# Inverse power-of-two factors for queries and keys in an attention and expert kernel

## The chip, the cores and the metric

The kernel runs on one core of a Trainium2 chip. Its engines are TensorE (PE in the profile; PEld is its loading of weights), VectorE (DVE), ScalarE (ACT), GpSimd (POOL) and SyncE (SP), which issues most of the DMAs. The metric is the device time of one execution in microseconds.

## The reference

The input x (2048 rows of 512) is normalised by rows to xn, and two branches read xn. The result is `x + A(xn) + B(xn)`.

```python
def _A_ref(x, wq, wk, wv, wo):          # H = 32 heads, Dh = 16, one key and value head
    q = (x @ wq).reshape(B, S, H, Dh).transpose(0, 2, 1, 3)
    k = x @ wk
    v = x @ wv
    scores = jnp.einsum("bhqd,bkd->bhqk", q, k) * (Dh ** -0.5)
    p = softmax(scores, axis=-1)
    o = jnp.einsum("bhqk,bkd->bhqd", p, v)
    return o.transpose(0, 2, 1, 3).reshape(B, S, H * Dh) @ wo
```

Branch B projects xn for 32 expert heads, scores each half of a projection against 64 sub-keys, takes the best two of each half, forms the best two of 4096 experts, and adds up `softmax(score) * gelu(xn . u[e]) * v[e]` over heads and chosen experts.

## The kernel before

**Start.** The normalised rows are transposed in four groups of 512 rows. `transpose_group` (L182) transposes four 128x128 blocks on TensorE into one PSUM buffer, copies them on ScalarE to a rounded high part (L193), and VectorE subtracts to get the low part (L194). `key_products` (L208) multiplies a group with the key and value weights, twelve matmuls; ScalarE copies the product (L217), squares the keys (L219) and makes a scaled copy of them in fp16 (L221). `key_rows` (L224) subtracts for the low part of the keys (L226) and puts six DMAs in line that copy them into `kaug`. For each of four blocks of query columns, `queries` (L1360) runs `query_products` (L251, twelve matmuls), `query_sq` (L260, a square on ScalarE), whatever functions are passed as `between`, `query_high` (L265, the scaled fp16 copy on ScalarE) and `query_low` (L274, the low part on VectorE, with two stores). `query_products` alternates between two PSUM buffers, so a block waits until the block two before it has gone through `query_low`.

**The factors.** Queries and keys are stored in fp16, scaled by powers of two. `weight_squares` (L289) has ScalarE square the query and key weights with a sum along each row; `scale_factors` (L297) sums over partitions with one matmul (L301), takes the root on ScalarE, and gets `sqk` (one factor for queries, one for keys) and `soft`, which takes both factors back out and holds the 1/4 of the reference. The squares stand ahead of the first `transpose_group`, and `scale_factors` ahead of the first `key_products`.

**Attention.** There are 32 units (four blocks of 512 queries, eight groups of four heads). For each unit and each of 16 blocks of 128 keys, `scores` (L406) runs two matmuls twice into a PSUM buffer of 128x1024 (two of these exist), and ScalarE takes the exponential of each (L417) with `soft`, a tile of one value per partition, as its scale. `pv` (L419) multiplies the exponentials with the values. One step of `att_steps` (L1250) holds two key blocks, thus four exponentials.

**Experts, interleaved.** Between the scores of a step the program's order lays pieces of branch B: sub-key scores (L629) with the best values (L642, L644); gathers of expert rows by POOL (L1089), dot products (L1101) and sums (L1136) on VectorE for the first half of the rows; and for the second half a dense form. That one builds a matrix of gates from one-hot rows on VectorE (L890 to L893), with small matmuls (L923) and a copy on ScalarE (L928), and then multiplies all experts (L831, L969). The dense form runs twice, once for each of the last two groups of rows. The order of instructions on every engine is written out by the program; `spent` and the costs that `yield` returns set it, and no run changes it.

Of the kernel before, what the change touches and what calls it, by code (L numbers as in the profile page):

```python
# [11 lines left out]
F32 = mybir.dt.float32  # L12
F16 = mybir.dt.float16
F32R = mybir.dt.float32r
BF16 = mybir.dt.bfloat16
I32 = mybir.dt.int32
U32 = mybir.dt.uint32
AF = mybir.ActivationFunctionType
OP = mybir.AluOpType
AX = mybir.AxisListType  # L20
# [3 lines left out]
P = 128  # L24
# [3 lines left out]
DH = 16  # L28
# [4 lines left out]
KC = D // P  # L33
# [12 lines left out]
SCALE = DH ** -0.5  # L46
LIMIT2 = 25000.0
C_IN = 0.7978845608028654
C_CUB = 0.044715 * C_IN
TOP = 1024.0  # L50
MROW = 32768.0
EXPONENT = 0x7F800000
HOLD = 44
MOST = 4.0
UNIT = 0.235
# [3 lines left out]
def tile_kernel(ctx, tc, x, wq, wkv, wo, wqT, kT, uv, ub, vb, out):  # L59
    nc = tc.nc  # L60
    pool = lambda name, **kw: ctx.enter_context(tc.tile_pool(name=name, **kw))
    dram = pool("dram", bufs=1, space=DRAM)
    const = pool("const", bufs=1)
# [4 lines left out]
    start = start_stack.enter_context(tc.tile_pool(name="start", bufs=1))  # L68
# [23 lines left out]
    wkv_f = start.tile([P, KC, 32], F32, name="wkv_f")  # L92
# [5 lines left out]
    vaug = const.tile([P, NT, 32], F32, name="vaug")  # L98
# [6 lines left out]

    mrow = start.tile([2, 512], F16, name="mrow")
    nc.gpsimd.memset(mrow, MROW)
    blk = start.tile([P, 32], BF16, name="blk")
    blk_f = start.tile([P, 32], F32, name="blk_f")
    nc.gpsimd.memset(blk_f, 1.0)  # L110
# [13 lines left out]
    xtile = lambda name: ps.tile([P, 512], F32, name=name, tag="x", bufs=3)  # L124
    stile = lambda name: ps.tile([P, 2, 512], F32, name=name, tag="s")
# [24 lines left out]
    def norm_stats(g, js):  # L150
        if g not in MV:
            MV[g] = start.tile([P, GT, 2], F32, name="mv", bufs=2)
        for j in js:
            st = start.tile([P, 6], F32, name="st", bufs=2)
            nc.vector.bn_stats(st, XS[g][j])
            nc.vector.bn_aggr(MV[g][:, j, :], st)
        if js[-1] == GT - 1:
            v = start.tile([P, GT], F32, name="ve", bufs=2)
            nc.vector.tensor_scalar(v, MV[g][:, :, 1], 1e-5, None, op0=OP.add)
            sd = start.tile([P, GT], F32, name="sd", bufs=2)  # L160
            nc.scalar.activation(sd, v, AF.Sqrt)
            RS[g] = v, sd
# [19 lines left out]
    def transpose_group(g, ks=range(KC)):  # L182
        first = g < 1
        for k in ks:
            if first:
                xt = big.tile([P, 2, 512], F32R, name="xt", bufs=4)
                XT.append(xt)
            else:
                xt = start.tile([P, 2, 512], F32R, name="xtt", tag="xtt", bufs=6)
            p = xtile("ptr")  # L190
            for j in range(GT):
                nc.tensor.transpose(p[:, j * P:(j + 1) * P], XN[g * GT + j][:, k * P:(k + 1) * P], ident)
            nc.scalar.copy(xt[:, 0, :], p)  # L193
            nc.vector.tensor_tensor(out=xt[:, 1, :], in0=p, in1=xt[:, 0, :], op=OP.subtract)  # L194
            XK.setdefault(g, []).append(xt)
            if not first:
                BULK.append(lambda k=k, xt=xt: nc.sync.dma_start(d_xt[g - 1][k], raw(xt[:])))
# [2 lines left out]

    FIRST = ((0, 0), (1, 0), (0, 1))
    sqk = const.tile([P, 2], F32, name="sqk")
    soft = const.tile([P, 1], F32, name="soft")
    qmax = const.tile([P, NGRP], F32, name="qmax")
    kmax = small.tile([32, NGRP], F32, name="kmax", bufs=1)
    KV, SQ, PQ, PK, QT = {}, {}, {}, {}, {}

    def key_products(g):  # L208
        p = stile("pkv")[:32, 0, :]
        n = 0  # L210
        for a, b in FIRST:
            for k in range(KC):
                w = (wkv_h, wkv_l)[a]
                nc.tensor.matmul(p, w[:, k, :], XK[g][k][:, b, :], start=n == 0, stop=n == 11)
                n += 1
        kv = big.tile([32, 512], F32, name="kv", tag="wk", bufs=NWK)
        nc.scalar.copy(kv, p)  # L217
        sq = start.tile([16, 512], BF16, name="ksq", tag="sq", bufs=3)
        nc.scalar.activation(sq, kv[:16, :], AF.Square)  # L219
        kh = big.tile([32, 2, 512], F16, name="kh", tag="wk", bufs=NWK)  # L220
        nc.scalar.activation(kh[:, 0, :], kv, AF.Copy, scale=sqk[:32, 1:2])  # L221
        KV[g] = kv, kh, sq

    def key_rows(g):  # L224
        kv, kh, sq = KV[g]
        nc.vector.scalar_tensor_tensor(kh[:, 1, :], kv, sqk[:32, 1:2], kh[:, 0, :], op0=OP.mult, op1=OP.subtract)  # L226
        c = slice(g * 512, (g + 1) * 512)

        def copies():
            for base in (0, 64):  # L230
                nc.sync.dma_start(kaug[base:base + 16, c], kh[:16, 0, :])
                nc.sync.dma_start(kaug[base + 16:base + 32, c], kh[:16, 1, :])
                nc.sync.dma_start(kaug[base + 32:base + 48, c], kh[:16, 0, :])

        store(copies)
# [7 lines left out]
                              pt[:, :P].rearrange("p (c n) -> p c n", n=32)[:, :, DH:])  # L243

    def key_squares(g):
        kv, kh, sq = KV.pop(g)
        p = xtile("pks")
        nc.tensor.matmul(p[:32, :], blk[:16, 0:1].to_broadcast([16, 32]), sq, start=True, stop=True)
        nc.vector.reduce_max(kmax[:, g:g + 1], p[:32, :], axis=AX.X)
# [37 lines left out]
            nc.vector.reduce_max(qmax[:, g:g + 1], PK.pop(g), axis=AX.X)  # L287

    def weight_squares():  # L289
        cols = PK["cols"] = start.tile([P, 3], F32, name="cols")  # L290
        waste = stile("pws")
        for i in range(2):
            nc.scalar.activation(waste, wraws[i], AF.Square, accum_out=cols[:, i:i + 1])
        nc.scalar.activation(waste[:, 0, :KC * DH].rearrange("p (k n) -> p k n", k=KC), wkv_f[:, :, :DH], AF.Square,
                             accum_out=cols[:, 2:3])

    def scale_factors():  # L297

        ones = vaug[:, :4, :].rearrange("p t n -> p (t n)")
        p = xtile("pws")  # L300
        nc.tensor.matmul(p[:, :3], ones, PK.pop("cols"), start=True, stop=True)  # L301
        total = start.tile([P, 2], F32, name="total")
        nc.vector.tensor_copy(total, p[:, 1:3])
        nc.vector.tensor_add(total[:, 0:1], total[:, 0:1], p[:, 0:1])
        root = start.tile([P, 2], F32, name="root")
        nc.vector.tensor_scalar(total, total, 1e-36, None, op0=OP.max)
        nc.scalar.activation(root, total, AF.Sqrt)
        nc.vector.reciprocal(root, root)
        nc.vector.tensor_single_scalar(root.bitcast(I32), root.bitcast(I32), EXPONENT, op=OP.bitwise_and)
        nc.vector.tensor_scalar(sqk, root, TOP, None, op0=OP.mult)  # L310
        back = start.tile([P, 2], F32, name="back")
        nc.vector.reciprocal(back, sqk)
        nc.vector.scalar_tensor_tensor(soft, back[:, 0:1], SCALE, back[:, 1:2], op0=OP.mult, op1=OP.mult)

    def zero_m():
        z = gtile(F16)
# [87 lines left out]
    PT, PV = {}, {}  # L404

    def scores(u, kc, i):  # L406
        p = stile("sc")
        for b in range(2):
            o = 64 * b
            nc.tensor.matmul(p[:, b, :], kaug[o:o + 64, kc * P:(kc + 1) * P], QA[u][o:o + 64, i, :],  # L410
                             start=True, stop=True)
        if (u, kc, i) not in PT:
            if late[0] is None:
                PT[u, kc, i] = gtile(F32, (P, 2, 512), "pt")
            else:
                PT[u, kc, i] = late[0].tile([P, 2, 512], F32, name="pt", tag="pt", bufs=6)
        nc.scalar.activation(PT[u, kc, i], p, AF.Exp, scale=soft)  # L417

    def pv(u, kc):  # L419
        if kc == 0:  # L420
# [114 lines left out]
    def out_ready():  # L535
        return PWO and GT * QB[PWO[0][0]] + PWO[0][1] in LIVE
# [713 lines left out]
    def att_steps(d, mid, fill):  # L1250
# [25 lines left out]
        if 0 < i < STEPS:  # L1276
            scores(u, kc + 1, 0)
            scores(u, kc + 1, 1)
        if out_ready() and (i % 128 >= HOLD and PWO[0][0] != 1 or i % 128 >= 32 and i % 4 == 0 and PWO[0][0] == 1):
            block_out()  # L1280
# [39 lines left out]
    with tc.manual_schedule(engines=ENGINES):  # L1320
        load_group(0)
        nc.sync.dma_start(wkv_f, wkv.rearrange("(k p) n -> p k n", p=P))
        wraws = []
# [19 lines left out]
                                                    in1=wqs[k][:, 0, :], op=OP.subtract)  # L1343
        for k in range(KC):
            nc.scalar.copy(wqs[k][:, 0, :], wraws[k // 2][:, k % 2, :])
        weight_squares()
        norm_apply(0)
        wq_half(0)
        wq_half(1)
        transpose_group(0)  # L1350
        wq_half(2)
        wq_half(3)
        scale_factors()

        def stores(bulk=0):
            run(STORES)
            for _ in range(min(bulk, len(BULK))):
                BULK.pop(0)()

        def queries(g, r, *between):  # L1360
            stores(2)
            query_products(g, r)
            query_sq(g, r)
            for fn in between:
                fn()
            query_high(g, r)
            query_low(g, r)

        key_products(0)
        queries(0, 0, lambda: norm_stats(1, range(2)), lambda: key_rows(0))  # L1370
        queries(0, 1, lambda: value_rows(0), lambda: query_squares(0, 0), lambda: norm_stats(1, range(2, GT)))
        queries(0, 2, lambda: key_squares(0), lambda: query_squares(0, 1), lambda: norm_apply(1))
# [190 lines left out]
```

## Time and profile before

| | us |
|---|---|
| median of 3 runs | 1848.32 |
| lowest and highest run | 1840.08, 1848.66 |
| the profiled execution | 1845.24 |
| its span | 1843.5 |
| mean granted clock of TensorE | 0.996 of full speed |

The profile is of one execution. The span runs from its first to its last instruction on the core. Rows name the line, the engine, the operation, and the tile written and read; "busy" is the time in which an engine executed. A row of waits says which engine's line stood idle and whose result ended the wait.

### The profile page before, as it was taken

To read this page: it belongs to the slowest core of one execution; us is meant where nothing else is said; L and a number is where in the kernel's file an instruction comes from. 1 tells how busy PE (TensorE), PEld (TensorE's weight loads), DVE (VectorE), ACT (ScalarE), POOL (GpSimd) and SP (SyncE) were. 2 spreads that over 40 slices of the span, in tenths; PEclk is the share of its full clock that TensorE was granted. 3 is DMA by queue.
4 is the path that set the end of the run, shared out by engine and by line. 5 is a ranking of instruction groups with operands and counts; after the bars stand their busy time and mean duration, and the time that the engine had idled before them with its cause. 6 is when DMAs were issued, how large, how long until landed. Compare 5 with 4: busy or idle time off the path is not lost.

```text
span 1843.5 us, 34938 instructions
## 1 busy us (share of the span) xinstructions
PE 1762.1 (96%) x10991; PEld 885.1 (48%) x10991; DVE 1627.5 (88%) x6386; ACT 1376.5 (75%) x1752; POOL 701.4 (38%) x921
## 2 busy tenths in 40 slices
PE   7999999999998889999999999999987899999998
PEld 4644444455554334555555544555543344555553
DVE  6749988999899967999999897899989778999994
ACT  4367766666668997888888666666689888888884
POOL 1124544435442113344344453345421124444430
PEclk9999999999999999999999999999999999999999
DMA  7489897996754767888899996877626759998882
GB/s 267 187 300 371 300 334 239 353 323 240 238 186 140 239 227 223 276 265 290 289 294 323 350 317 220 292 250 245 229 90 220 250 181 295 284 304 282 290 276 98
DMA packets 243705, 478.31 MB, mean 259 GB/s; under 512 B 93748, under 2 KB 117316, under 8 KB 243516
## 3 DMA queue, kind: packets, MB, share of 16 engines
q0 software_dynamic: 73728, 268.47, 43.2%
q1 hardware_dynamic: 169372, 206.93, 33.8%
q8 instruction: 87, 1.43, 0.3%
q14 instruction: 102, 0.84, 0.1%
q10 hardware_dynamic: 416, 0.66, 0.1%
HBM read 419.94 MB, written 51.15 MB: 256 GB/s over the span
## 4 chain that ended last, share of the span: by engine, by line
PE 67%; DVE 8%; ACT 7%; DMA 5%; issue 4%; SPq 1%; POOL 1%; another core or an unknown queue 0%; ACTq 0%; DVEq 0%; POOLq 0%
PE pv L427 19%; PE psc L629 17%; PE sc L410 12%; PE pact L831 8%; PE pout L969 7%; ACT pt L417 5%; PE pwo L525 2%; DVE xa L1136 2%; PE pw L581 1%; DVE g L1101 1%; DVE oh L890 1%; DVE i L644 1%; DMA wk<-dw 1%; DMA g<-in_uv_dram,idx 1%; ACT gst L928 1%
## 5 line engine op out<-in xcount | busy, mean ns | idle before, releaser
L417 ACT ACTIVATE pt<-sc,soft 128x1024 f32<-128x1024 f32 x1024 | 1087.9, 1123 | 336.4 <-PE sc L410 277.3
L1089 POOL DMA_INDIRECT g<-in_uv_dram,idx x512 | 563.3, 1100 | 909.5 <-DVE xa L1136 425.2
L427 PE MATMUL pv<-pt,vaug 128*32 128x512 f32 x4096 | 496.4, 602 | 0.0
L629 PE MATMUL psc<-wk,xt 128*128 128x512 f32 x1536 | 391.5, 402 | 2.7 <-DVE wk L591 1.0
L410 PE MATMUL sc<-qa,kaug 64*128 64x512 f16 x2048 | 338.6, 383 | 43.4 <-ACT pt L417 37.9
L1136 DVE SCALAR_TENSOR_TENSOR xa<-g,w,xa 128x512 f32<-128x512 f32 x512 | 374.6, 751 | 0.1
L1101 DVE CUSTOM_DVE_ANT_0 g<-g,xa 128x512 f32<-128x512 f32 x512 | 337.1, 689 | 5.6 <-DMA g<-in_uv_dram,idx 5.4
L629 PEld LDWEIGHTS psc<-wk,xt 128*128 128x128 f32 x1536 | 277.7, 188 | 96.3 <-issue 34.7
L410 PEld LDWEIGHTS <-kaug 64*128 64x128 f16 x2048 | 87.2, 94 | 403.9 <-issue 400.8
L427 PEld LDWEIGHTS pv<-pt,vaug 128*32 128x32 f32 x4096 | 107.4, 109 | 254.3 <-issue 254.3
L644 DVE FIND_INDEX8 i<-m,psc 128x8 uint32<-128x64 f32 x1024 | 207.7, 233 | 0.6 <-issue 0.6
L969 PE MATMUL pout<-wk,wd 128*128 128x512 f32 x768 | 194.9, 401 | 2.0 <-DVE gy L1012 1.1
L831 PE MATMUL pact<-xt,wk 128*128 128x512 f32 x768 | 196.5, 400 | 0.0
L969 PEld LDWEIGHTS pout<-wk,wd 128*128 128x128 f32 x768 | 140.7, 188 | 43.9 <-issue 5.6
L831 PEld LDWEIGHTS pact<-xt,wk 128*128 128x128 f32 x768 | 139.3, 188 | 42.4 <-issue 13.2
L642 DVE MAX8 m<-psc 128x8 f32<-128x64 f32 x1024 | 146.8, 221 | 14.2 <-PE psc L629 13.0
L796 DVE TENSOR_TENSOR wk<-rw,wk 128x512 fp32r<-128x512 f32 x128 | 85.9, 691 | 9.7 <-ACT wk L795 9.7
L972 DVE TENSOR_TENSOR da<-da,pout 128x512 f32<-128x512 f32 x128 | 83.0, 688 | 5.4 <-PE pout L969 5.4
L644 DVE MATCH_VALUE_LOAD i<-m,psc 128x8 f32 x1024 | 82.9, 81 | 0.0
L890 DVE TENSOR_TENSOR oh<-oh 128x2048 f16<-128x2048 f16 x64 | 78.1, 1220 | 3.4 <-ACT oh L857 1.6
L795 ACT CAST wk<-rw 128x512 fp32r<-128x512 f32 x128 | 74.3, 634 | 0.0
L1124 DVE SCALAR_TENSOR_TENSOR w<-gth,ga 128x4 f32<-128x4 f32 x128 | 20.9, 163 | 54.0 <-ACT gth L1117 48.8
(178 smaller groups left out, 1333.3 us busy)
## 6 DMA issues: line engine op xcount, KB each, us to landing
wk<-dw SPq DMA_DIRECT2D x96, 512.0 KB
wqt<-in_wqT_dram SPq DMA_DIRECT2D x32, 512.0 KB
dw<-wk SPq DMA_DIRECT2D x32, 512.0 KB
rw<-in_ub_dram SPq DMA_DIRECT2D x64, 256.0 KB
rw<-in_vb_dram SPq DMA_DIRECT2D x64, 256.0 KB
gy<-dg SPq DMA_DIRECT2D x64, 256.0 KB
dg<-gst SPq DMA_DIRECT2D x14, 928.0 KB
g<-in_uv_dram,idx POOLq DMA_INDIRECT x512
```

Source lines behind the costliest of these rows:

```text
L410: nc.tensor.matmul(p[:, b, :], kaug[o:o + 64, kc * P:(kc + 1) * P], QA[u][o:o + 64, i, :], start=True, stop=True)
L417: nc.scalar.activation(PT[u, kc, i], p, AF.Exp, scale=soft)
L427: nc.tensor.matmul(PV[u][32 * j:32 * j + 32, :], vaug[:, kc, :], pt[:, b, :], start=kc == 0, stop=kc == 15)
L629: nc.tensor.matmul(p, XT[k][:, a, j * P:(j + 1) * P], WC[n_][k][:, bb, :], start=n == 0, stop=n == 11)
L642: nc.vector.max(m8[:, jb, s, :], p[:, s * E:(s + 1) * E])
L644: nc.vector.max_index(i8[:, jb, s, :], m8[:, jb, s, :], p[:, s * E:(s + 1) * E])
L831: nc.tensor.matmul(p, us[:, a, k * P:(k + 1) * P], XT[k][:, c, :], start=n == 0, stop=n == 11)
L890: nc.vector.tensor_tensor(out=oa, in0=num(P), in1=bc(0, tb, P), op=OP.is_equal)
L969: nc.tensor.matmul(p, wd[0][:, a, j * P:(j + 1) * P], vs[:, c, :], start=n == 0, stop=n == 5)
L1089: nc.gpsimd.indirect_dma_start(out=gt, out_offset=None, in_=uv, in_offset=bass.IndirectOffsetOnAxis(ap=IDX[ph, c, ti][:, s:s + 1], axis=0))
L1101: nc.vector.tensor_tensor_reduce(u, u, XN[TPH * ph + ti], scale=1.0, scalar=0.0, op0=OP.mult, op1=OP.add, accum_out=a[:, i:i + 1])
L1136: nc.vector.scalar_tensor_tensor(acc, v, w[:, i:i + 1], acc, op0=OP.mult, op1=OP.add)
```

## The change

`weight_squares` writes the squares themselves, as bf16, without sums; it runs after the transposes of the first group. `scale_factors` runs after the first `key_products`, and sums the squares over the 512 input features with eight matmuls against a matrix of ones, so each column of the weights gets the square of its norm. It takes the largest of the query columns and of the key columns, and the fourth root of their ratio, cut to a power of two, is the queries' factor; the keys' factor is its inverse. `soft` is gone, and the exponential's scale is the number `SCALE` = 0.25. The scaled copy of the keys moves from `key_products` into `key_rows`, so in ScalarE's order it stands behind the square of the first query block.

```diff
-TOP = 1024.0
+LEAST = 1e-18
...
+    ones = start.tile([P, P], BF16, name="ones")
+    nc.gpsimd.memset(ones, 1.0)
...
-    soft = const.tile([P, 1], F32, name="soft")
...
         nc.scalar.activation(sq, kv[:16, :], AF.Square)
+        KV[g] = kv, sq
+
+    def key_rows(g):
+        kv = KV[g][0]
         kh = big.tile([32, 2, 512], F16, name="kh", tag="wk", bufs=NWK)
         nc.scalar.activation(kh[:, 0, :], kv, AF.Copy, scale=sqk[:32, 1:2])
-        KV[g] = kv, kh, sq
-
-    def key_rows(g):
-        kv, kh, sq = KV[g]
...
     def weight_squares():
-        cols = PK["cols"] = start.tile([P, 3], F32, name="cols")
-        waste = stile("pws")
+        sq = PK["wsq"] = start.tile([P, KC, 512], BF16, name="wsq")
         for i in range(2):
-            nc.scalar.activation(waste, wraws[i], AF.Square, accum_out=cols[:, i:i + 1])
-        nc.scalar.activation(waste[:, 0, :KC * DH].rearrange("p (k n) -> p k n", k=KC), wkv_f[:, :, :DH], AF.Square,
-                             accum_out=cols[:, 2:3])
+            nc.scalar.activation(sq[:, 2 * i:2 * i + 2, :], wraws[i], AF.Square)
+        sk = PK["ksq"] = start.tile([P, KC, DH], BF16, name="wksq")
+        nc.scalar.activation(sk, wkv_f[:, :, :DH], AF.Square)
 
     def scale_factors():
 
-        ones = vaug[:, :4, :].rearrange("p t n -> p (t n)")
-        p = xtile("pws")
-        nc.tensor.matmul(p[:, :3], ones, PK.pop("cols"), start=True, stop=True)
-        total = start.tile([P, 2], F32, name="total")
-        nc.vector.tensor_copy(total, p[:, 1:3])
-        nc.vector.tensor_add(total[:, 0:1], total[:, 0:1], p[:, 0:1])
-        root = start.tile([P, 2], F32, name="root")
-        nc.vector.tensor_scalar(total, total, 1e-36, None, op0=OP.max)
-        nc.scalar.activation(root, total, AF.Sqrt)
-        nc.vector.reciprocal(root, root)
-        nc.vector.tensor_single_scalar(root.bitcast(I32), root.bitcast(I32), EXPONENT, op=OP.bitwise_and)
-        nc.vector.tensor_scalar(sqk, root, TOP, None, op0=OP.mult)
-        back = start.tile([P, 2], F32, name="back")
-        nc.vector.reciprocal(back, sqk)
-        nc.vector.scalar_tensor_tensor(soft, back[:, 0:1], SCALE, back[:, 1:2], op0=OP.mult, op1=OP.mult)
+        sq, sk = PK.pop("wsq"), PK.pop("ksq")
+        p, q = xtile("pws"), xtile("pwk")
+        for k in range(KC):
+            nc.tensor.matmul(p, ones, sq[:, k, :], start=k == 0, stop=k == KC - 1)
+        for k in range(KC):
+            nc.tensor.matmul(q[:, :DH], ones, sk[:, k, :], start=k == 0, stop=k == KC - 1)
+        most = start.tile([P, 2], F32, name="most")
+        nc.vector.reduce_max(most[:, 0:1], p, axis=AX.X)
+        nc.vector.reduce_max(most[:, 1:2], q[:, :DH], axis=AX.X)
+        nc.vector.tensor_scalar(most, most, LEAST, None, op0=OP.max)
+        root = start.tile([P, 1], F32, name="root")
+        nc.vector.reciprocal(root, most[:, 0:1])
+        nc.vector.tensor_mul(root, root, most[:, 1:2])
+        nc.scalar.activation(root, root, AF.Sqrt)
+        nc.scalar.activation(root, root, AF.Sqrt)
+        nc.vector.tensor_single_scalar(sqk[:, 0:1].bitcast(I32), root.bitcast(I32), EXPONENT, op=OP.bitwise_and)
+        nc.vector.reciprocal(sqk[:, 1:2], sqk[:, 0:1])
...
-        nc.scalar.activation(PT[u, kc, i], p, AF.Exp, scale=soft)
+        nc.scalar.activation(PT[u, kc, i], p, AF.Exp, scale=SCALE)
...
-        weight_squares()
         norm_apply(0)
         wq_half(0)
         wq_half(1)
         transpose_group(0)
+        weight_squares()
         wq_half(2)
         wq_half(3)
-        scale_factors()
...
         key_products(0)
+        scale_factors()
         queries(0, 0, lambda: norm_stats(1, range(2)), lambda: key_rows(0))
```

More of the change, by code (lines that the diff above doesn't have):

```diff
@@ L245, in key_squares @@
     def key_squares(g):
-        kv, kh, sq = KV.pop(g)
+        kv, sq = KV.pop(g)
         p = xtile("pks")
```

## The prediction

> **What bounds the kernel now.** I read the page first, then the busy time by stage, then who waited for whom. Of the page, the span, PE's row and the costliest group carry the argument:
>
> ```profile
> span 1843.5 us, 34938 instructions
> PE 1762.1 (96%) x10991; PEld 885.1 (48%) x10991; DVE 1627.5 (88%) x6386; ACT 1376.5 (75%) x1752; POOL 701.4 (38%) x921
> L417 ACT ACTIVATE pt<-sc,soft 128x1024 f32<-128x1024 f32 x1024 | 1087.9, 1123 | 336.4 <-PE sc L410 277.3
> ```
>
> TensorE is busy 96% of the span and ScalarE 75%. The exponential, the line whose scale changes, is 1024 instructions and four fifths of ScalarE's work, but ScalarE sat idle 336.4 us before it, mostly waiting for TensorE. An average hides stages, so I asked for the busy time in stretches (start:end, length, then busy us and count for each engine, granted clock, DMA share):
>
> ```profile
> 900.00:1000.00 100.00, 99.18 (x583) 51.84 (x582) 98.25 (x232) 85.09 (x115) 45.51 (x39) 1.00 0.89 286
> 1100.00:1200.00 100.00, 100.00 (x568) 48.70 (x567) 85.70 (x505) 65.32 (x72) 37.01 (x56) 1.00 0.77 262
> ...
> 575.00:665.00 90.00, 72.77 (x891) 30.51 (x889) 84.30 (x165) 86.76 (x110) 16.93 (x14) 0.98 0.55 186
> 1375.00:1463.00 88.00, 71.96 (x814) 30.48 (x814) 76.13 (x152) 83.55 (x106) 16.21 (x14) 0.98 0.64 216
> ```
>
> The columns are PE, PEld, DVE, ACT, POOL. The first two rows stand for most of the span: TensorE is full, and a cheaper exponential buys nothing there. The last two rows are the stages that build the one-hot gates (L890 to L928). There ScalarE is the fullest (86.76 of 90, 83.55 of 88), VectorE is close behind (84.30 and 76.13), and TensorE is not the bound. The waits agree; the first row is the whole span, the others are the two one-hot stages (us in total, times, longest):
>
> ```profile
> PE sc L410 <- ACT pt L417: 37.9, 70, 1.4
> ```
> ```profile
> PE sc L410 <- ACT pt L417: 14.5, 25, 1.0
> ```
> ```profile
> PE sc L410 <- ACT pt L417: 13.6, 24, 1.0
> ```
>
> TensorE waits 37.9 us for exponentials in all, and 28.1 us of that lies in these two stages. What is left elsewhere is 9.8 us in 21 waits. The chain of waits, by line, differs between the two stages:
>
> ```profile
> by line: ACT pt L417 43.7%; issue 28.7%; ACT gst L928 11.1%; PE pv L427 9.7%; PE sc L410 3.5%; another core or an unknown queue 1.7%; ACT gth L1117 0.7%; ACT wk L795 0.7%; ACT gy L847 0.2%; ACT e L435 0.2%; ACTq L928 0.2%; ACTq L417 0.1%; A
> ```
> ```profile
> by line: DVE oh L890 24.5%; ACT pt L417 10.4%; DVE oh L893 8.2%; issue 7.9%; DVE xa L1136 7.7%; DVE oh L892 7.4%; DVE g L1101 6.2%; PE pv L427 3.2%; SPq L763 3.1%; DMA dg<-gst 3.0%; DMA ot<-e 2.8%; ACT gst L928 2.6%; DMA qa<-dm 2.2%; SPq L7
> ```
>
> In the first, the chain is ScalarE's; in the second, over half of it (24.5+8.2+7.7+7.4+6.2 = 54%) is VectorE's.
>
> **Part 1: the exponential's scale becomes an immediate.** The trace has no exponential of this shape with an immediate scale, so I bound the saving. Groups with their shapes kept apart:
>
> ```profile
> L271 ACT ACTIVATE qt<-pq,sqk 128x512 f16<-128x512 f32 x15 | 10.2, 680 | 0.0
> L262 ACT ACTIVATE qsq<-pq 128x512 bf16<-128x512 f32 x16 | 9.6, 597 | 33.2 <-PE pq L256 33.2
> L293 ACT ACTIVATE pws<-g 128x1024 f32<-128x1024 f32 x2 | 2.0, 1024 | 0.0
> ```
>
> L271 reads its scale from a tile and L262 does not; same source, same shape, 680 against 597 ns, so 83 ns. At 1024 columns, 1123 against 1024 ns (L293, no scale tile) is 99 ns. These are durations; what counts in a full queue is the distance from start to start:
>
> ```profile
> 612.92 2.19 ACT L417 ACTIVATE pt<-sc,soft 128x1024 f32<-128x1024 f32 x2
> 614.93 0.65 ACT L928 COPY gst<-pg 128x512 f32<-128x512 f32 x1
> ...
> 617.49 0.59 ACT L928 COPY gst<-pg 128x512 f32<-128x512 f32 x1
> 617.95 2.14 ACT L417 ACTIVATE pt<-sc,soft 128x1024 f32<-128x1024 f32 x2
> ```
> ```profile
> 10.90 1.02 ACT L293 ACTIVATE pws<-g 128x1024 f32<-128x1024 f32 x1
> 11.86 0.18 ACT L293 ACTIVATION_READ_ACCUMULATOR pws<-g 128x1 f32 x1
> ```
>
> Two exponentials take 614.93 - 612.92 = 2.01 us, 1.005 each. The L293 row without a scale tile gives way after 0.96, which makes the saving 0.045. A copy of 512 columns gives way after 0.46 (617.49 to 617.95); with 512 further columns at (1024 - 597)/512 = 0.83 ns it would be 0.887, which makes it 0.118. I take the middle, 0.083, which is also the difference of the 512-column rows. ScalarE loses 1024 x 0.083 = 85 us of work, and the question is how much of that is anyone's wait.
>
> The Trainium skill, "ScalarE: Activation LUTs", section "What ACT_TABLE_LOAD costs", says that each pointer operand adds about 93 ns, and also that back-to-back activations overlap by about that much. By the first sentence the trace agrees (83 and 99 ns), and by the figure ScalarE would lose an estimated 95 us. By the second the saving could vanish in a full queue, which is a rival below.
>
> *First one-hot stage.* It holds the exponentials of this group, and the second stage those of the next:
>
> ```profile
> L417 ACT ACTIVATE pt<-sc,soft 128x1024 f32<-128x1024 f32 x68 | 73.5, 1174 | 3.2 <-remote 1.6 <-PE sc L410 1.5
> ```
> ```profile
> L417 ACT ACTIVATE pt<-sc,soft 128x1024 f32<-128x1024 f32 x65 | 70.6, 1187 | 4.5 <-PE sc L410 2.6 <-remote 1.7
> ```
>
> 68 x 0.083 = 5.6 us off ScalarE, whose queue is the chain. VectorE is idle only 90 - 84.30 = 5.7 us there, in pieces, so it becomes late next; I take 3.5 (bounds 0 and 68 x 0.118 = 8.0). *Second stage.* 65 x 0.083 = 5.4 us off ScalarE, but half the chain is VectorE's, which does not get faster; I take 1.5 (bounds 0 and 7.7). *Elsewhere.* 21 waits, each shortened by about one exponential's 0.09: at most 1.9, I take 1.0; in the rest of the span TensorE's own work hides the gain. Sum of part 1: -6.0 us, bounds 0 and -17.6.
>
> **Part 2: the squares later, the factors from matmuls.** In the start-up, by engine:
>
> ```profile
> 10.11 3.46 PE L192 MATMUL ptr<-ident,xa 128*128 128x128 f32 x12 [10.11 <-DVE xa L177]
> 14.86 1.12 PE L192 MATMUL ptr<-ident,xa 128*128 128x128 f32 x4 [1.28 <-DVE xt L194]
> 15.77 0.43 PE L301 MATMUL pws<-cols,vaug 128*128 128x3 f32 x2
> 16.05 1.89 PE L214 MATMUL pkv<-xt,wkv_h 128*32 128x512 f32 x4
> ...
> 19.19 1.09 PE L214 MATMUL pkv<-xt,wkv_h 128*32 128x512 f32 x4
> 20.12 4.71 PE L256 MATMUL pq<-xt,wqs 128*128 128x512 f32 x20
> ```
> ```profile
> 13.51 1.54 ACT L193 CAST xt<-ptr 128x512 fp32r<-128x512 f32 x3
> ...
> 23.05 0.60 ACT L262 ACTIVATE qsq<-pq 128x512 bf16<-128x512 f32 x1 [0.88 <-PE pq L256]
> ```
>
> Today the squares hold ScalarE from 10.90 to 13.51, and the first casts of the transposed input stand behind them; VectorE's subtractions follow, and TensorE's last four transposes wait 1.28 us for a buffer. With the squares moved behind the casts, those transposes can follow the first twelve at about 13.6 instead of 14.86: 1.3 us sooner, and the removed pair of L301 gives 0.28 more (15.77 to 16.05). The key products then run from about 14.5 to 18.7 (4.23 us, 16.05 to 20.28, as now). Behind them come four new 128x512 matmuls and four of 16 columns. Rows for these and for the reduction that reads them:
>
> ```profile
> 36.80 0.39 PE L285 MATMUL pqs<-qsq,blk 128*32 128x512 bf16 x1
> ```
> ```profile
> 58.13 0.68 DVE L249 TENSOR_REDUCE kmax<-pks 32x1 f32<-32x512 f32 x1 [0.34 <-PE pks L248]
> ```
> ```profile
> 18.82 0.17 DVE L306 TENSOR_SCALAR total<-total 128x2 f32<-128x2 f32 x1
> 19.25 0.17 DVE L308 RECIPROCAL root<-root 128x2 f32<-128x2 f32 x1 [0.27 <-ACT root L307]
> ```
>
> The four long ones take 4 x 0.27 (19.19 row, in a stream) to 4 x 0.39, the short ones perhaps 0.2 together: 1.3 to 1.8 us. The query products therefore start at 20.0 to 20.5 against 20.12. The factors need both reductions (0.68 and about 0.25), five small VectorE steps at 0.17 and a handover each, say 0.2, and two roots on ScalarE (0.43 from 18.82 to 19.25 with its handovers, the second about 0.2): 2.6 us after some 20, ready near 22.7. They are first read behind the square of the first query block, which ends at 23.65 today, so the query products and that square hide them; without this cover each late us would stand on the query path.
>
> The scaled key copy (L221, like L271 a copy with a scale tile) moves behind that square, so it delays the query's scaled copy by up to 0.68 us in each of the four groups. Its six DMAs on SP and its VectorE subtraction move with it, from behind the key copy to behind the first query square (23.65), and the stores of the queries queue behind the six; no score reads either until the attention starts, two further groups later. In the second group the subtraction also has the normalisation of the third group behind it on VectorE, and then two query subtractions, which free the buffer of the third query product; this may cost a few tenths once. The bf16 ones are one memset on POOL at the start, and TensorE reads them only at about 18.7. I take +0.5 us for all of part 2 (bounds -1.4, the transposes' gain kept, and +2.0, the matmuls and a late factor paid in full).
>
> **Sum.** -6.0 + 0.5 = -5.5 us. The profiled execution took 1845.24 us (span 1843.5 and 1.7 around it), so its like would take 1839.7. The median of before is 1848.32, 3.1 above it, and 1848.32 - 5.5 = 1842.8. I predict 1841, between the two.
>
> **The rivals.** *A: hidden anyway.* The pointer's fetch overlaps the preceding activation, or VectorE is late at once in both stages; then part 1 is 0 and part 2 decides: 1844 to 1847 beside the profiled execution, up to 1850 beside the median. For it: VectorE's 84.30 of 90. Against it: 1.005 against 0.96 and 0.887. *B: ScalarE sets more than the waits show.* The upper bounds hold: -17.6 - 1.4 = -19 gives 1826, half of it 1836. For it: the chain of the first stage. Against it: the second stage's chain. *C: every pointer counts*, -85 us, 1760: only if ScalarE were the bound everywhere, which the 336.4 us of idle time denies. *D: slower, by TensorE's clock.* The granted clock dips in the one-hot stages:
>
> ```profile
> 630.00:640.00 10.00, 6.94 (x102) 1.00 0.81 270
> 640.00:650.00 10.00, 9.10 (x96) 0.83 0.55 207
> ...
> 1420.00:1430.00 10.00, 8.15 (x86) 0.83 0.75 255
> ```
> ```profile
> 1364.90 3.02 PE L427 MATMUL pv<-pt,vaug 128*32 128x512 f32 x16
> ...
> 1370.83 1.92 PE L427 MATMUL pv<-pt,vaug 128*32 128x512 f32 x16
> ```
>
> Such a dip costs 3.02 - 1.92 = 1.1 us a burst (the last pair of rows: the burst of 16 in a dip of the second stage, and the next one). If the new rhythm made it dip in more of these steps, each would add 1.1: beyond five it eats the gain, and at 17 of some 34 steps the result is 1841 + 19 = 1860. For it: TensorE falls to 6.94 of 10 just ahead of one dip. Against it: a shorter exponential shortens these gaps. The Trainium skill, "TensorE: Matmul & The Clock Gate", "Part 1: The HAM clock gate (the "warmup" mystery)", puts such dips down to idle windows; the row ahead of the dip agrees.
>
> **How the numbers follow.** About 0.5% (9.2 us) is what a measurement here tells from no change. Forecast, -2 to -9 us: 0.48. A: 0.26. B, -9 to -19: 0.17. D: 0.07. C: 0.02. Faster by over 0.5%: B, C and the forecast's edge, 0.24. Slower: D and a trace of A, 0.09. Within: 0.67. The range runs from B's bound, 1826, to A's worst beside the median, 1850; C and D are left out.
>
> **What would show it.** The exponential's mean near 1030 ns and pairs 1.84 to 1.92 us apart from start to start; ScalarE near 1290 us; both one-hot stages shorter by 1 to 5 us with VectorE above 95% of the first; query products starting at 20 to 20.5 and no ScalarE wait for the factors; every other stage as long as before. The prediction is wrong if the stages with a full TensorE change length, or if the clock dips often.

## The result, and the profile after

The changed kernel takes 1823.3 us, median of 6 runs (1820.98 to 1826.76); the kernel before took 1847.99 beside it (6 runs). The ratio is 0.9881, 95% interval 0.9858 to 0.9903. That is 22 us less, where the prediction said 5.5 less and gave a range that ended at 1826.

The page of the kernel after:

```profile
span 1821.5 us, 34944 instructions
...
PE 1743.2 (96%) x10997; PEld 880.0 (48%) x10997; DVE 1625.8 (89%) x6385; ACT 1290.0 (71%) x1750; POOL 698.9 (38%) x922
...
L419 ACT ACTIVATE pt<-sc 128x1024 f32<-128x1024 f32 x1024 | 995.9, 1030 | 379.5 <-PE sc L412 317.8
...
L412 PE MATMUL sc<-qa,kaug 64*128 64x512 f16 x2048 | 319.6, 382 | 27.6 <-ACT pt L419 22.5
```

And one row of the page of before that the prediction did not look at:

```profile
L410 PE MATMUL sc<-qa,kaug 64*128 64x512 f16 x2048 | 338.6, 383 | 43.4 <-ACT pt L417 37.9
```

The exponential went from 1123 to 1030 ns, as forecast, and ScalarE from 1376.5 to 1290.0 us. But look at the score matmuls: the same 2048 of them, of the same mean length (383 and 382 ns), were "busy" 338.6 us before and 319.6 us after. The page of before had booked up to 19 us of TensorE's waiting as work.

To see where, I cut the execution at the first burst of the values' matmuls (`pv`) of each of the 256 attention steps, as the timeline gives their starts. Steps 64 to 82 and 184 to 200 hold the one-hot stages:

| us | to the first burst | steps 0-64 | 64-82 | 82-184 | 184-200 | 200-255 | the rest |
|---|---|---|---|---|---|---|---|
| before | 121.15 | 450.30 | 97.14 | 696.31 | 87.05 | 373.57 | 18.0 |
| after | 119.50 | 444.05 | 92.08 | 694.76 | 82.75 | 370.77 | 17.6 |
| difference | -1.65 | -6.25 | -5.06 | -1.55 | -4.30 | -2.80 | -0.4 |

In this pair of executions the one-hot stages give 9.4 us, and the stages in which TensorE was thought full give 10.6. Single executions scatter by a few us a stage; the experiments below repeat the comparison. One step of such a stage, TensorE alone (start, length, line, tiles, shape, count), before:

```profile
1221.87 0.61 PE L410 MATMUL sc<-qa,kaug 64*128 64x512 f16 x4
1222.41 1.92 PE L427 MATMUL pv<-pt,vaug 128*32 128x512 f32 x16
1224.26 0.66 PE L410 MATMUL sc<-qa,kaug 64*128 64x512 f16 x4
1224.85 3.72 PE L629 MATMUL psc<-wk,xt 128*128 128x512 f32 x15
1228.50 0.61 PE L410 MATMUL sc<-qa,kaug 64*128 64x512 f16 x4
1229.04 1.50 PE L427 MATMUL pv<-pt,vaug 128*32 128x512 f32 x12
```

and after:

```profile
1209.28 1.93 PE L429 MATMUL pv<-pt,vaug 128*32 128x512 f32 x16
1211.14 0.61 PE L412 MATMUL sc<-qa,kaug 64*128 64x512 f16 x4
1211.67 3.73 PE L631 MATMUL psc<-wk,xt 128*128 128x512 f32 x15
1215.33 0.60 PE L412 MATMUL sc<-qa,kaug 64*128 64x512 f16 x4
1215.87 1.50 PE L429 MATMUL pv<-pt,vaug 128*32 128x512 f32 x12
```

From burst to burst the step takes 1229.04 - 1222.41 = 6.63 us before and 1215.87 - 1209.28 = 6.59 after. The difference sits in the score matmuls behind the burst: the next line starts 1224.85 - 1224.26 = 0.59 us after them before, and 0.53 after. The weight loads (PEld) show what happens there, first before, then after:

```profile
1224.26 0.11 PEld L410 LDWEIGHTS <-kaug 64*128 64x128 f16 x3 [0.84 <-issue]
1224.53 0.09 PEld L410 LDWEIGHTS <-kaug 64*128 64x128 f16 x1 [0.17 <-issue]
```
```profile
1211.13 0.19 PEld L412 LDWEIGHTS <-kaug 64*128 64x128 f16 x4 [0.84 <-issue]
```

Before, the fourth load stands apart, at 1224.53; after, all four go together. The exponentials say why, before and after:

```profile
1222.36 2.12 ACT L417 ACTIVATE pt<-sc,soft 128x1024 f32<-128x1024 f32 x2 [2.80 <-PE sc L410]
```
```profile
1209.23 1.94 ACT L419 ACTIVATE pt<-sc 128x1024 f32<-128x1024 f32 x2 [2.93 <-issue]
```

The last two score matmuls write the buffer that the second of these exponentials reads. Before, it ends at 1222.36 + 2.12 = 1224.48, and the late load follows 0.05 us behind it, at 1224.53. After, it ends at 1211.17, ahead of the turn of those two matmuls, which start 1211.36 - 1211.14 = 0.22 us into their group:

```profile
1211.36 0.38 PE L412 MATMUL sc<-qa,kaug 64*128 64x512 f16 x2
```

So TensorE stalled by 0.04 to 0.06 us in such a step, and no wait and no idle time was booked: with a modelled length of 383 ns, while the four follow one another within 0.53, a matmul's bar reaches over so short a gap. It is not one step alone. Of the 441 such groups of four outside the one-hot stages, 222 took more than 0.55 us until the next line started before the change, about one in every step, and 25 after. The waits before the weight loads of the scores, over the whole span, before and after (us in total, times, longest), are another witness:

```profile
PEld L410 <- issue: 400.8, 776, 1.7
```
```profile
PEld L412 <- issue: 341.3, 539, 2.0
```

237 waits fewer. The stretches of the same stages still say "full" after (PE, PEld, DVE, ACT, POOL), and the one-hot stages are close on two engines:

```profile
1200.00:1300.00 100.00, 100.00 (x591) 52.80 (x590) 96.32 (x624) 59.73 (x73) 49.87 (x100) 1.00 0.71 242
563.00:656.00 93.00, 77.23 (x959) 33.41 (x962) 89.13 (x177) 88.81 (x120) 16.99 (x15) 1.00 0.60 200
1350.00:1433.00 83.00, 67.59 (x866) 29.50 (x865) 81.73 (x161) 77.53 (x106) 16.22 (x14) 0.99 0.63 209
```

The start-up, TensorE after the change:

```profile
10.06 4.19 PE L194 MATMUL ptr<-ident,xa 128*128 128x128 f32 x16 [10.06 <-DVE xa L179]
14.01 1.34 PE L215 MATMUL pkv<-xt,wkv_h 128*32 128x512 f32 x4
...
17.05 1.04 PE L302 MATMUL pws<-wsq,ones 128*128 128x512 bf16 x4
17.92 0.25 PE L304 MATMUL pwk<-wksq,ones 128*128 128x16 bf16 x4
18.02 5.69 PE L257 MATMUL pq<-xt,wqs 128*128 128x512 f32 x24
```

The sixteen transposes run without the pause, and the query products start at 18.02 instead of 20.12. The trace's record of TensorE's granted clock has its first entry of full speed at 13.99 us here, just ahead of the key products, and at 18.89 before, where they started at 16.05.

### The profile page after: what moved, and what is told of

Read it like the earlier page. It is cut to its first block, busy times and chain, and to the rows that moved or that the text cites. A ratio compares the mean times of both kernels' runs of the same rounds, so it can differ in the third digit from the quotient of the medians.

```text
span 1821.5 us, 34944 instructions
## 1 busy us (share of the span) xinstructions
PE 1743.2 (96%) x10997; PEld 880.0 (48%) x10997; DVE 1625.8 (89%) x6385; ACT 1290.0 (71%) x1750; POOL 698.9 (38%) x922
## 4 chain that ended last, share of the span: by engine, by line
PE 48%; DVE 32%; DMA 6%; issue 4%; ACT 3%; POOL 1%; SPq 1%; DVEq 0%; ACTq 0%; POOLq 0%
PE psc L631 16%; PE pv L429 13%; PE sc L412 8%; DVE xa L1138 7%; DVE g L1103 6%; PE pact L833 3%; DVE oh L892 3%; PE pout L971 3%; DVE i L646 2%; DVE da L974 2%; PE pwo L527 2%; ACT pt L419 2%; DVE wk L798 1%; PE pw L583 1%; DMA rsb<-dinv 1%
## 5 line engine op out<-in xcount | busy, mean ns | idle before, releaser
L419 ACT ACTIVATE pt<-sc 128x1024 f32<-128x1024 f32 x1024 | 995.9, 1030 | 379.5 <-PE sc L412 317.8
L412 PE MATMUL sc<-qa,kaug 64*128 64x512 f16 x2048 | 319.6, 382 | 27.6 <-ACT pt L419 22.5
L412 PEld LDWEIGHTS <-kaug 64*128 64x128 f16 x2048 | 82.4, 94 | 346.2 <-issue 341.3
L646 DVE MATCH_VALUE_LOAD i<-m,psc 128x8 f32 x1024 | 77.7, 76 | 0.0
L690 POOL CAST fi<-i 128x64 f32<-128x64 uint32 x32 | 9.0, 281 | 136.7 <-DVE i L646 131.8
```

Of the source, the lines that this page charges most:

```text
L419: nc.scalar.activation(PT[u, kc, i], p, AF.Exp, scale=SCALE)
L646: nc.vector.max_index(i8[:, jb, s, :], m8[:, jb, s, :], p[:, s * E:(s + 1) * E])
```

## The experiments

**Theory S**: the whole gain but some 2 us is the exponential's 93 ns; in the one-hot stages ScalarE was the bound, and in the others the second exponential ended just behind its cover and stalled TensorE by 0.05 us a step, which the profile counts as busy. It saturates: once the pair ends inside its cover, a shorter exponential gives nothing more. **Rival L**: the time follows ScalarE's work in proportion, 20 us for 85. **Rival M**: the moved start-up shifts the phase of all that follows. **The prediction's own**: TensorE-bound stages gain nothing. Each ratio below is to the kernel before, measured beside that run on the same chip.

### One part undone: the tile as scale again

```diff
...
-        nc.scalar.activation(PT[u, kc, i], p, AF.Exp, scale=SCALE)
+        nc.scalar.activation(PT[u, kc, i], p, AF.Exp, scale=soft)
```

The lines left out make `soft` a tile that holds 0.25.

> The changed kernel, but the exponential reads its scale 0.25 from a tile again. Theory S (the exponential's 93 ns are the gain, part of it in stalls of TensorE that the trace counts as busy): the steps of the TensorE-bound stages go back from 6.585 to 6.63 us and the one-hot steps from about 4.7 to about 5.1; only the start-up's 1.7 us stay, so about 1846, ratio to before 0.999. Rival M (the moved start-up changes the phase of everything behind it, the exponential matters little): stays near 1823, ratio 0.988. Rival L (a fixed share of every us taken off ScalarE): about 1846 as well.

1843.38 us, ratio 0.9981 (0.9972 to 0.9990); the median step of the stage from 145 to 183 is back at 6.63. Rival M falls: the start-up alone is worth 2 to 5 us.

### One part alone: the number in the kernel before

```diff
-        nc.scalar.activation(PT[u, kc, i], p, AF.Exp, scale=soft)
+        nc.scalar.activation(PT[u, kc, i], p, AF.Exp, scale=SCALE / 4096)
```

> The kernel before, with only the exponential's scale replaced by the number that soft holds for these inputs (0.25/4096). Theory S: everything but the start-up's 1.7 us: about 1827, ratio 0.989, TensorE-bound steps 6.585, first query products at 20.1 as before. Rival M: stays within 3 us of before.

1822.4 us, ratio 0.9868 (0.9851 to 0.9885): the whole of the change's gain, within the intervals, without its start-up (first query products at 19.91), and 5 us more than S's 1827. The step is 6.56, where S said 6.585: the score matmuls behind the burst take 0.54 us to the next line, as in the kernel after, but the fifteen expert matmuls take 3.63 instead of 3.66. Why they differ is open; the exponentials are as long in both kernels.

### Half of the exponentials

```diff
...
-        nc.scalar.activation(PT[u, kc, i], p, AF.Exp, scale=SCALE)
+        nc.scalar.activation(PT[u, kc, i], p, AF.Exp, scale=soft if i else SCALE)
```

> The changed kernel, but the second exponential of each pair reads its scale from a tile; half of the 85 us on ScalarE are given back. Theory S: a pair then takes about 1.93 us from start to start, which still ends inside the values' burst of 1.85 us and the matmuls around it, so TensorE-bound steps stay at 6.585; one-hot steps lose about half of their gain (4.9). About 1828, ratio 0.990. Rival L (linear in ScalarE's time): half of the 20 us is lost, steps at 6.61, about 1834, ratio 0.994.

1828.09 us, ratio 0.9895 (0.9878 to 0.9912), as S said and 6 us under L. Outside the one-hot stages the 221 steps took 1511.1 us, against 1509.6 after and 1520.2 before: with half of the saving they keep all but 1.5 of the gain. The median step of the stage from 145 to 183 is 6.55, with the same 3.63 us for the fifteen expert matmuls. The one-hot stages took 177.0 (174.8 after, 184.2 before).

### The number in the one-hot steps alone

```diff
...
-        nc.scalar.activation(PT[u, kc, i], p, AF.Exp, scale=SCALE)
+        d = 8 * u + kc // 2
+        nc.scalar.activation(PT[u, kc, i], p, AF.Exp, scale=SCALE if 64 <= d < 83 or 184 <= d < 201 else soft)
```

> The changed kernel with the number as scale in the one-hot steps alone (64 to 82 and 184 to 200), the tile everywhere else. Theory S: these steps keep their 8.6 us, the TensorE-bound steps go back to 6.63 and lose about 10 us: about 1836, ratio 0.994. Rival L: 85 us of ScalarE's time fall back by the share of exponentials outside, 7/8 of 20 us lost: about 1844, ratio 0.998. Rival of the prediction (TensorE-bound stages gain nothing): stays within 2 us of the changed kernel.

1837.8 us, ratio 0.9952 (0.9937 to 0.9967). The one-hot stages took 174.8 us, all of their gain; the others 1525.4, none of theirs. So the stages that the prediction put at 1 us hold a real gain, and it is the larger part: by the medians on this chip, the number in the one-hot steps alone is worth 1843.38 - 1837.80 = 5.6 us beside the tile everywhere.

The executions of these runs show how far one pair can be trusted. Outside the one-hot stages, the four with the tile there (before, this run and the tile as scale, profiled twice) took 1520.2 to 1525.4 us, and the four with the number (after, the number in the kernel before, and the early squares below, twice) 1507.2 to 1512.8. On average that is 13 us, or 0.06 a step, and in the table's three stages 4.5, 4.5 and 4.0; the -1.55 of its steps 82-184 is the scatter of one execution. The first one-hot stage took 95.3 to 97.3 us with the tile and 92.0 to 94.3 with the number, the second 85.2 to 87.1 and 81.0 to 85.2: on average 4 and 3 us (four and six executions, those with more cover below among them).

### The cost doubled: scale and bias from tiles

```diff
...
-        nc.scalar.activation(PT[u, kc, i], p, AF.Exp, scale=SCALE)
+        nc.scalar.activation(PT[u, kc, i], p, AF.Exp, scale=soft, bias=shift)
```

The lines left out make `soft`, a tile that holds 0.25, and `shift`, a tile of zeros.

> The changed kernel, but the exponential reads its scale and its zero bias from tiles: the suspected cost is doubled. Theory S: each exponential some 0.09 us longer again, a pair 0.18; nothing is left to cover that in the TensorE-bound steps, so they go from 6.63 with one tile to about 6.81, and the one-hot steps from 5.1 to about 5.4: 1843 + 205 x 0.18 + 34 x 0.33 = about 1891, ratio 1.024; the loss from the second tile is about twice that from the first. Rival L (linear): a second 20 us, 1864, ratio 1.009. Rival: both operands are fetched together, no change from one tile, 1843.

1894.72 us, ratio 1.024 (1.0218 to 1.0262). The exponential's group, one step on TensorE, and the exponentials and weight loads of the step behind it:

```profile
L423 ACT ACTIVATE pt<-sc,shift,soft 128x1024 f32<-128x1024 f32 x1024 | 1180.3, 1212 | 303.6 <-PE sc L416 240.7 <-issue 25.9 <-PE psc L635 17.4
```
```profile
1267.13 1.92 PE L433 MATMUL pv<-pt,vaug 128*32 128x512 f32 x16
1268.99 0.84 PE L416 MATMUL sc<-qa,kaug 64*128 64x512 f16 x4
1269.76 3.70 PE L635 MATMUL psc<-wk,xt 128*128 128x512 f32 x15
...
1273.93 1.92 PE L433 MATMUL pv<-pt,vaug 128*32 128x512 f32 x16
```
```profile
1273.89 2.30 ACT L423 ACTIVATE pt<-sc,shift,soft 128x1024 f32<-128x1024 f32 x2 [2.11 <-PE sc L416]
```
```profile
1275.78 0.11 PEld L416 LDWEIGHTS <-kaug 64*128 64x128 f16 x3 [0.84 <-issue]
1276.24 0.09 PEld L416 LDWEIGHTS <-kaug 64*128 64x128 f16 x1 [0.35 <-issue]
```

The second tile adds 1212 - 1122 = 90 ns, and the step is 1273.93 - 1267.13 = 6.80 us. The loss sits behind the burst: 0.77 us from the score matmuls to the next line, 0.24 more than after. The pair of exponentials ends at 1273.89 + 2.30 = 1276.19 and the late load stands at 1276.24, again 0.05 us behind it: the exponential sets it. The first tile cost 6.63 - 6.59 = 0.04 us a step and the second, of equal price, 0.17 (at the place itself 0.06 and 0.18): the corner that S names, and no straight line.

### More cover in place of a shorter exponential

```diff
...
         mid()
+        if dense_on[0] != 2:
+            run_scores(until=min(aim, spent[0] + 0.7))
         if 0 < i < STEPS:
             scores(u, kc + 1, 0)
```

In the kernel before:

> The kernel before, tile scale and all, but in the steps outside the one-hot build a piece of about 0.7 us of the expert scores goes ahead of the step's second pair of score matmuls, which so get more time after the first pair. Theory S: TensorE no longer stalls on the exponentials, these steps fall from 6.63 to 6.56 to 6.59 with exponentials as long as before; one-hot steps unchanged: about 1847 - 9 = 1838, ratio 0.995. If the steps are shorter in the changed kernel for another reason (a faster sequence on TensorE, less traffic), they stay at 6.63: 1847 or slower.

In the changed kernel:

> The changed kernel with the same piece moved ahead. Theory S: there is no stall left to take away, steps stay at 6.56 to 6.59: within 3 us of the changed kernel, 1820 to 1826. If stalls of the same kind remain elsewhere (steps of other lengths), a few us faster than the changed kernel.

Both missed: 1882.23 us, ratio 1.0183 (1.0164 to 1.0202), and 1866.55, ratio 1.0097 (1.0077 to 1.0117). One step of each, with the tile and with the number:

```profile
1242.89 1.92 PE L427 MATMUL pv<-pt,vaug 128*32 128x512 f32 x16
1244.75 0.96 PE L629 MATMUL psc<-wk,xt 128*128 128x512 f32 x3
1245.64 0.61 PE L410 MATMUL sc<-qa,kaug 64*128 64x512 f16 x4
1246.17 3.02 PE L629 MATMUL psc<-wk,xt 128*128 128x512 f32 x12
...
1249.66 1.92 PE L427 MATMUL pv<-pt,vaug 128*32 128x512 f32 x16
```
```profile
1242.96 0.97 PE L631 MATMUL psc<-wk,xt 128*128 128x512 f32 x3
1243.86 0.61 PE L412 MATMUL sc<-qa,kaug 64*128 64x512 f16 x4
1244.40 3.02 PE L631 MATMUL psc<-wk,xt 128*128 128x512 f32 x12
```

Cutting the fifteen expert matmuls in two costs more than the stall: 0.89 + 2.95 us for the three and the twelve, against 3.65 for fifteen in a row, so 6.77 a step. But the pair shows what it was made for. The score matmuls take 0.53 and 0.54 us, with the tile and with the number, and outside the one-hot stages the two kernels take 1550.8 and 1548.4 us: the tile's price there has fallen from 10.6 us (13 on average) to 2.5 by cover alone, which is within the scatter of single executions.

### The squares ahead of the transposes again

```diff
+        weight_squares()
         norm_apply(0)
...
         transpose_group(0)
-        weight_squares()
```

> The changed kernel with the weights' squares back ahead of the first transposes on ScalarE; the factors stay where they are. If the earlier first casts are what the start-up gains, the first query products go from 18.0 back to 20 or later (20.5 with the new matmuls) and the first burst of values from 119.5 to about 121.5. If the gain comes from elsewhere in the start-up, the first query products stay near 18.

The query products started at 20.14 and the first burst at 121.61, so the earlier casts are what the start-up gains. Over all runs, the query products started at 17.0 to 19.4 us in the nine executions with the squares behind the transposes and at 19.9 to 22.0 in the five with them ahead, and the first burst came 1.9 us earlier on average (118.5 to 121.1 against 120.9 to 123.0). TensorE's rows of this run:

```profile
14.03 1.12 PE L194 MATMUL ptr<-ident,xa 128*128 128x128 f32 x4 [1.17 <-DVE xt L196]
14.79 2.05 PE L215 MATMUL pkv<-xt,wkv_h 128*32 128x512 f32 x4
```

The pause is back, and the first four key products take 2.05 us instead of 1.34. The pause is not what sets their time: in two other runs the transposes ran without it and the four still took 1.88 us (half of the exponentials) and 2.06 (three quarters of the slots, below). What goes with their time in all runs is the granted clock. Where its record reaches full speed ahead of them, they take 1.34 us; where that comes 0.3 to 1.1 us after their start, 1.44 to 1.67; and where it comes 1.5 us or more after it, 1.88 to 2.06. Full speed came at 12.8 to 17.0 us in the executions with the squares behind the transposes, and at 18.1 to 22.0 in those with them ahead. The one execution took 1833.18 us, 8 more than this explains, so I ran it again, with the tile beside it:

> The same kernel as the run with the early squares, whose one look took 1833.2: 10 us over the changed kernel where only 2 were expected from the start-up. If the other 8 are chance (a long transfer and dips of TensorE's clock in that one execution), the median is 1825 to 1827, ratio about 0.989 to 0.990. If the squares' place decides more than the start-up, it stays near 1833, ratio 0.993.

> The changed kernel with the tile as scale again, beside the early squares on one chip: the start-up alone against before, 0.998 as in the first run if the start-up is worth 2 to 4 us; 0.994 or less if its place decides 8 us more.

1822.26 us, ratio 0.9886 (0.9867 to 0.9906), and 1838.66, ratio 0.9980 (0.9969 to 0.9991). The 8 us did not come back in four executions, so they were chance of that one. What the start-up is worth in the end cannot be told from these ratios beyond "some us": it shows beside the tile (0.998) and not beside the number (0.9868 without it, 0.9881 with it).

### Fewer expert slots in the one-hot steps

```diff
-   (..., 0, 1.0, 1.5, 0.5)[dense_on[0]]
+   (..., 0, 0.5, 1.5, 0.5)[dense_on[0]]
```

> The changed kernel, but in the one-hot steps the program lays half as many expert slots (a dot product and a sum on VectorE) and makes them up later. If VectorE is what bounds these steps now, they go from 4.7 to 5.2 us down to 4.66, some 5 us less in each of the two stages, and the slots made up elsewhere cost 0 to 10 us in steps where VectorE is also nearly full: 1814 to 1824, ratio 0.982 to 0.988. If ScalarE still bounds them, no change in these steps: 1823 or slower.

> The same with three quarters of the slots: half of the effect, 1818 to 1824 if VectorE bounds the one-hot steps.

1849.63 us, ratio 1.0018 (1.0007 to 1.0030), and 1839.28, ratio 0.9960 (0.9946 to 0.9974): both slower than the change, and outside the forecasts for a VectorE bound. (The second run has 0.75 in place of 0.5.) The slots made up later cost 22 and 12 us in the steps 200 to 255. And the one-hot stages did not get shorter in sum: 178.7 and 177.8 us against 174.8. The first of them with half of the slots:

```profile
563.00:660.00 97.00, 79.96 (x976) 33.77 (x976) 78.56 (x145) 90.83 (x122) 8.05 (x7) 0.98 0.46 159
```

VectorE is down to 78.56 of 97, ScalarE still at 90.83. Part of the stage's length is one step of 9.36 us. The other 17 take 84.4 us against 86.8 after, but most of that is one step, which was 6.51 us long after and 4.73 here; the shortest steps stay at 4.66 us, as after. So the floor of these steps is not VectorE's. No version here beats the change by more than the intervals.

## Why the prediction was wrong

- **The exponential's saving** was right: 93 ns in length (99 and 83 were the rows' answers). A pair back to back, from the start of the first to the end of the second, fell from 2.12 to 1.94 us, 0.09 each, a little over the 0.083 taken. Rival A did not occur. Two exponentials in a row do overlap by about 0.1 us (a pair takes 1.94 us, two alone 2 x 1.03 = 2.06), but they did so with the tile as well (2.12 against 2 x 1.123 = 2.25), so the overlap hides nothing of the tile's price, and the second tile's 90 ns are paid in full too. The Trainium skill, "ScalarE: Activation LUTs", "What ACT_TABLE_LOAD costs", gives 93 ns for each pointer operand, and these runs agree twice.
- **The step that failed** is "in the rest of the span TensorE's own work hides the gain", with its "at most 1.9, I take 1.0". It measured 10.6 in the pair of executions above and 13 on average over eight, and the prediction's own sign of being wrong, stages with a full TensorE that change length, came true. The bound counted 21 booked waits and took 99 and 100% busy for no stall at all. The trace of before could have warned. Matmuls' ends in it are modelled, and the cover can be computed from the step above: the pair of exponentials ends 1224.48 - 1221.87 = 2.61 us after the score matmuls start, and its buffer is due after 0.54 for these, 1.85 for the burst and 0.22 for the next two, 2.61 in all. That left nothing for the handover, which takes 0.05; after the change 1211.36 - 1211.17 = 0.19 us are left for it.
- **One-hot stages.** The mechanism was right. In the pair of executions above the gain was 5.1 us where the prediction took 3.5, and 4.3 where it took 1.5; over all executions kept it was about 4 and 3, and 5.6 for both by medians. So the first size was about right and the second too small. The second was given only a part since its chain ran over VectorE, but in both stages alike the commonest gain of a step is 0.33 to 0.36 us (15 of the 34 steps of this pair), which is the whole of four exponentials (4 x 0.09). The other steps scatter, from 1.7 us shorter to 2.3 us longer; what keeps their sum below 68 x 0.083 = 5.6 and 65 x 0.083 = 5.4 is not shown.
- **Start-up.** +0.5 predicted, -1.65 measured in this pair (-1.9 on average), 0.25 below its lower bound. The transposes' gain was right (14.01 against some 14.5 for the first key product). The mis-sized term is the key products, put at 4.23 us "as now"; they took 17.05 - 14.01 = 3.04, the first four 1.34 us instead of 1.89, with TensorE's clock at full speed from 13.99 us instead of 18.89. The prediction took their time as fixed. The factors were ready at about 20.35 and the square that covers them ended at 21.63, so nothing waited for them.
- **Rival B** had the right words, that ScalarE sets more than the waits show, but still put the stages outside the one-hot ones at 1.9 us at most, from the booked waits; the measured -22 lies beyond its end of -19. **Rival D** did not occur: the clock's mean was 0.998, against 0.996. Its reading of the dip as an idle stretch was loose, too: in the row ahead of it TensorE was busy 6.94 of 10 us, and its longest pause there was 0.93.

## What to carry to other kernels

Before calling an engine's full stretch a floor, take one repeated step, add up its groups from start to start, and hold the time of every hand-over against the work that covers it; a stall shorter than a modelled matmul shows in no busy share, only in the start of a late weight load or in a step a few hundredths too long. Such a cost has a corner: here the first 93 ns cost 0.04 us a step, the next 90 ns 0.17, and past the corner the other way nothing. Where two engines are both near full, a chain that runs over one of them is a weak reason to discount work taken off the other: look at the steps that repeat.

## What the runs showed of the hardware

- An activation's scale from a tile costs 93 ns at 1024 columns (1030 to 1123), and a bias from a tile as well another 90 (1122 to 1212). In a full queue both are paid: a pair of exponentials spans 1.94, 2.12 and 2.30 us.
- A score matmul that waits for an exponential to free its buffer starts its weight load 0.05 us after the exponential's end (1224.48 to 1224.53, 1276.19 to 1276.24).
- Fifteen 512-column matmuls in a row take 3.65 us; cut into three and twelve with other matmuls between, 3.84.
- The first four key products take 1.34 us where the trace's granted clock is at full speed before they start, and 1.88 to 2.06 where it gets there 1.5 us or more after. It got there at 12.8 to 17.0 us where TensorE's transposes paused for at most 0.3 us and at 18.1 to 22.0 where they paused for 1.2 to 2.4; that the pause delays the clock was not tested by itself.
